# A transformer block, forward and backward, on one core: another hand-set order of the same 1948 operations, and other addresses for their buffers

## The chip, the core and the metric

The kernel runs on one core of a Trainium2 chip. The core has five engines that each work through a queue of their own in order: TensorE (PE in the profile: matmuls, with its weight loads listed as PEld), VectorE (DVE), ScalarE (ACT), GpSimd (POOL) and SyncE (SP), which only issues transfers (DMAs). An instruction that waits for a semaphore holds up everything behind it on its own engine, and nothing on the others until they need its result. The metric is the device time of one execution in microseconds (us).

## What is computed

One pre-LN transformer block on x of 2048 x 512 (S x D), and the gradients of its inputs. The attention has 32 heads of 16, and each position looks at W = 8 positions, 2 apart, behind itself. The feed-forward part has 1792 columns.

```
def _A_ref(x, wqkv, wo):
    W, dil = 8, 2
    ...
    idx = pos[:, None] - off[None, :]
    ...
    logits = jnp.einsum("bhsd,bhswd->bhsw", q, kg) * scale
    ...
    o = jnp.einsum("bhsw,bhswd->bhsd", attn, vg)
    ...
h = x + _A_ref(_layernorm(x, axis=-1), A_wqkv, A_wo)
h2 = h + _B_ref(_layernorm(h, axis=-1), B_w1, B_b1, B_w2, B_b2)
...
_out, _vjp = jax.vjp(_f, A_x, A_wqkv, A_wo, B_w1, B_b1, B_w2, B_b2)
_grads = _vjp(grad_out)
```

The outputs are h2 and the gradients of x, wqkv, wo, w1, b1, w2 and b2.

## The kernel before

**Tiling and stages.** The 2048 positions are cut into four chunks of 512, called chunk 0 to 3 here; the kernel works on them in the order 0, 2, 1, 3 from the attention on. A chunk passes through these stages, all of them interleaved with those of other chunks: load of `xt`; statistics (L360, L361), reciprocal deviation by POOL (L373) and the shift `nm` by DVE (L376); normalization on ACT into `ln`; a DMA that transposes `ln` into `ln1T` (L291); the products with the weights for q and k (L616, in 32-column matmuls) and for v (L268 or L270); evictions from PSUM by ACT (L297: `qt`, `kt`, `tmv`); the band products of q and k on DVE (`prf`, L468, four to a chunk) and their sums by PE (L476); the maximum on DVE (`mx`, L682), its subtraction by PE (L268 or L270, named by `nident`), the exponential on ACT (`e`, L689), its sum by PE (L694), the reciprocal on DVE (`r`, L699), the weights `attn` (L701) and their transposed form `cfo` (L486); the band products with v on DVE (`prbo`, L507, four to a chunk), their sums by PE (L516) and the evictions `ost` (L521); a turn by PE (L532); the product with wo; the first residual `h` on DVE (L739); the second normalization; and the feed-forward products (`ln2T,w` then `w,gl`). In the backward half the same four kinds of band products stand as `prb`, `prbq`, `prbk` and `prbv`, and the gradient of x leaves DVE as `gx` (L559) over `jk`, `u` and `gyr`. The weight gradients are matmuls over all positions, evicted by ACT into `wgs`, `wgso` and `wgsq`, and stored.

**What sets the order.** `Plan` (L55 on) first records all operations, without issuing them: `pl.op` notes the engine, the buffers that are read and written and from them which operation must follow which. `Plan.emit` then issues them in the sequence of the table `ORDER`, a permutation of the 1948 numbers; each engine's queue is the part of it that falls to that engine. There is no scheduler at work beyond that table. A second table, `HOMES`, gives each buffer its address: a place in SBUF in units of 64 bytes, or one of the eight PSUM banks. Two buffers may have the same address one after the other. Then the first operation that writes the later one waits until the last one that uses the earlier one has ended; this is called a wait for an address below.

**What the order also decides.** A matmul of 128 columns is issued as four of 32 columns where the operations beside it are of the 32-column kind, so that PE does not change between the two kinds of layout. `emit` finds those stretches (`quad`), and `mmul` issues them:

```
if pl.quad:
    for a in range(4):
        T.matmul(out[32 * a:32 * a + 32, :], lhsT=l[:, 32 * a:32 * a + 32], rhs=r, start=start, stop=stop, skip_group_check=True)
else:
    T.matmul(out, lhsT=l, rhs=r, start=start, stop=stop, skip_group_check=True)
```

L268 is the first of these two calls and L270 the second, so one and the same product may have either line. SP's queue holds nearly all transfers: loads (L282), stores (L287, L445) and transposes (L291); the gathers of the neighbouring positions (L460) are issued by POOL.

Of the kernel before, what the change touches and what calls it, by code (L numbers as in the profile page):

```python
# [159 lines left out]
def kernel(  # L160
# [1026 lines left out]
    10, 24, 0, 25, 1, 8, 12, 11, 23, 14, 15, 69, 17, 29, 19, 20, 50, 22, 9, 26, 16, 51, 13, 52, 30, 53, 42, 27, 54, 252, 43, 39, 172, 55, 2, 18, 31,  # L1187
    61, 3, 44, 46, 28, 4, 32, 5, 45, 47, 56, 57, 355, 59, 64, 66, 48, 49, 67, 174, 65, 62, 60, 63, 68, 146, 171, 75, 173, 77, 78, 175, 148, 276, 76,
    176, 72, 353, 79, 274, 70, 38, 80, 177, 277, 178, 81, 71, 275, 181, 85, 86, 179, 278, 380, 279, 82, 180, 83, 379, 73, 84, 183, 6, 378, 87, 74,
    377, 88, 89, 280, 92, 381, 110, 382, 90, 284, 91, 105, 96, 283, 102, 93, 354, 97, 184, 94, 383, 112, 98, 99, 281, 95, 7, 100, 194, 597, 108, 195,  # L1190
    282, 101, 21, 189, 286, 196, 188, 114, 192, 250, 182, 190, 456, 109, 387, 111, 217, 191, 37, 386, 126, 285, 113, 193, 115, 185, 384, 116, 117,
    186, 385, 295, 215, 389, 187, 297, 118, 147, 288, 211, 595, 298, 58, 119, 294, 213, 299, 120, 296, 300, 201, 121, 122, 197, 128, 301, 127, 202,
    302, 129, 198, 203, 289, 199, 204, 292, 311, 290, 132, 200, 130, 291, 149, 403, 293, 303, 287, 140, 352, 305, 131, 251, 304, 404, 137, 306, 212,
    307, 214, 216, 205, 141, 314, 598, 133, 142, 138, 134, 218, 139, 405, 135, 318, 143, 136, 406, 408, 332, 480, 144, 152, 208, 316, 388, 156, 458,
    308, 407, 150, 320, 409, 315, 317, 319, 219, 321, 322, 153, 323, 220, 151, 324, 154, 157, 221, 161, 401, 155, 398, 325, 159, 397, 158, 160, 162,
    326, 163, 327, 164, 334, 333, 335, 338, 343, 400, 399, 391, 402, 395, 165, 392, 40, 168, 167, 394, 166, 222, 396, 170, 393, 336, 249, 337, 481,
    41, 414, 339, 596, 340, 341, 529, 342, 346, 507, 344, 508, 515, 345, 390, 223, 229, 347, 145, 224, 535, 348, 231, 351, 517, 419, 533, 518, 519,
    527, 520, 230, 530, 349, 421, 523, 350, 356, 536, 524, 505, 417, 528, 503, 534, 516, 509, 506, 525, 423, 504, 418, 526, 420, 510, 422, 484, 240,
    362, 360, 424, 511, 513, 485, 243, 514, 241, 415, 539, 242, 521, 358, 425, 483, 244, 363, 426, 245, 490, 543, 361, 411, 235, 544, 482, 427, 551,
    123, 246, 416, 232, 552, 599, 537, 236, 547, 247, 357, 410, 540, 364, 237, 494, 233, 359, 259, 234, 365, 531, 257, 366, 238, 367, 428, 239, 548,  # L1200
    368, 258, 369, 263, 255, 248, 370, 169, 253, 373, 374, 541, 256, 371, 262, 549, 372, 429, 559, 376, 254, 545, 261, 568, 435, 260, 553, 457, 264,
    610, 265, 560, 266, 225, 561, 604, 608, 546, 562, 550, 837, 861, 542, 845, 563, 329, 601, 267, 554, 862, 566, 835, 846, 564, 268, 269, 855, 836,
# [118 lines left out]
```

## Time and profile before

| | us |
|---|---|
| median of 3 runs (554.83 to 557.09) | 555.21 |
| the profiled execution, its own time | 555.56 |
| its span, first to last instruction | 553.8 |
| PE busy in it | 534.0 (96%) |
| DVE busy in it | 495.1 (89%) |
| ACT busy in it | 307.2 (55%) |
| POOL busy in it | 24.2 (4%) |
| mean granted TensorE clock, of 1 | 0.995 |

The span is 1.8 us shorter than the execution; times in the rows below are counted from the start of the span. A wait row such as "PE ps L516 <- DVE prbo L507: 3.2, 2, 1.6" says: matmuls of L516 that write PSUM waited for `prbo`, which DVE writes in L507, 3.2 us in all, in 2 places, at most 1.6 us in one. In a timeline, neighbours of one kind stand in one row with their number (x8), the first figure is the start and the second the length of all of them.

### The profile page before, as it was taken

The numbers are of one execution on the slowest core, as the hardware profiler recorded it, in microseconds if no ns is written. First come the engines' busy times: TensorE is split into PE (matmuls) and PEld (weight loads), VectorE is DVE, ScalarE is ACT, GpSimd is POOL, SyncE is SP. The second block draws the span as 40 slices with busy tenths as digits, with TensorE's granted clock in tenths as the row PEclk, the third lists the DMA queues.
The fourth block names the chain that finished last, engine by engine and source line by source line (L and its number), as shares of the span: only waits on it lengthen the run. The fifth ranks groups of instructions, "written<-read, shape, count | busy, mean of one in ns | idle before, by whom it ended". The sixth has DMA issues, their size and how long they took to land. (4 is left out here: it accounts for less than half of the span.)

```text
span 553.8 us, 12777 instructions
## 1 busy us (share of the span) xinstructions
PE 534.0 (96%) x5440; PEld 263.1 (48%) x5440; DVE 495.1 (89%) x649; ACT 307.2 (55%) x480; POOL 24.2 (4%) x38
## 2 busy tenths in 40 slices
PE   8989879999999999999999999999999999999996
PEld 4654434444544444444444445455445445545542
DVE  7999999999999999979993856788979999999993
ACT  3965466989989966987142323223133466652431
POOL 1200001020000100000000000000001001000000
PEclk9999999999999999999999999999999999999999
DMA  8999989997799488998999999999999999938346
GB/s 256 247 291 278 350 248 375 182 276 209 208 263 288 129 203 188 294 266 157 221 184 206 188 225 201 271 188 287 185 363 386 344 367 367 386 86 264 42 125 179
DMA packets 218121, 135.30 MB, mean 244 GB/s; under 512 B 168464, under 2 KB 213712, under 8 KB 216016
## 3 DMA queue, kind: packets, MB, share of 16 engines
q1 hardware_dynamic: 214752, 93.07, 72.8%
q0 software_dynamic: 3312, 41.42, 19.1%
q8 instruction: 42, 0.69, 0.5%
q14 instruction: 15, 0.12, 0.1%
HBM read 55.74 MB, written 39.40 MB: 172 GB/s over the span
## 5 line engine op out<-in xcount | busy, mean ns | idle before, releaser
L270 PE MATMUL ps<-goT,w2T 128*128 128x512 bf16 x220 | 52.5, 379 | 0.6 <-DVE xb L848 0.6
L270 PE MATMUL ps<-w1T,xb 128*128 128x512 bf16 x224 | 51.6, 379 | 0.0
L297 ACT CAST wgs<-ps 128x512 bf16<-128x512 f32 (+1 forms) x30 | 16.4, 558 | 63.1 <-PE ps L268 33.6
L270 PE MATMUL ps<-w,gl 128*128 128x512 bf16 x212 | 48.1, 379 | 0.0
L468 DVE TENSOR_TENSOR prb<-got,vw 128x4096 bf16<-128x4096 bf16 x16 | 36.3, 2282 | 12.2 <-PE ps L270 7.1
L270 PE MATMUL ps<-ln2T,w 128*128 128x512 bf16 x188 | 45.3, 389 | 0.3
L766 ACT ACTIVATE xb<-ps,b1c 128x512 bf16<-128x512 f32 x56 | 35.5, 695 | 10.6 <-PE ps L270 10.4
L848 DVE SCALAR_TENSOR_TENSOR xb<-xb,ps 128x512 bf16<-128x512 bf16 x56 | 36.6, 681 | 4.3 <-PE ps L270 3.8
L507 DVE TENSOR_TENSOR prbq<-Rq,cfq 128x4096 bf16<-128x4096 bf16 x16 | 35.8, 2280 | 2.5 <-PE ps L270 2.1
L507 DVE TENSOR_TENSOR prbv<-Rv,cfv 128x4096 bf16<-128x4096 bf16 x16 | 36.1, 2283 | 1.4 <-PE ps L516 1.3
L507 DVE TENSOR_TENSOR prbo<-Ro,cfo 128x4096 bf16<-128x4096 bf16 x16 | 36.0, 2286 | 0.6 <-PE ps L476 0.5
L507 DVE TENSOR_TENSOR prbk<-Rk,cfk 128x4096 bf16<-128x4096 bf16 x16 | 35.8, 2287 | 0.5 <-PE ps L268 0.3
L468 DVE TENSOR_TENSOR prf<-qt,kt 128x4096 bf16<-128x4096 bf16 x16 | 35.7, 2280 | 0.0
L270 PEld LDWEIGHTS <-xb 128*128 128x128 bf16 x224 | 21.9, 98 | 26.5 <-issue 0.2
L270 PEld LDWEIGHTS <-w2T 128*128 128x128 bf16 x220 | 21.5, 98 | 27.0 <-issue 1.4
L270 PEld LDWEIGHTS <-gl 128*128 128x128 bf16 x212 | 20.7, 98 | 24.6 <-issue 0.2
L616 PE MATMUL ps<-ln1T,wqk 128*32 128x512 bf16 x512 | 30.0, 382 | 1.1 <-ACT ln1T L297 1.1
L788 ACT ACTIVATE xb<-xb 128x2048 bf16<-128x2048 bf16 (+1 forms) x16 | 26.9, 1692 | 6.5 <-DVE xb L787 6.3
L270 PEld LDWEIGHTS <-w 128*128 128x128 bf16 x188 | 18.5, 100 | 23.8 <-issue 4.1
L268 PE MATMUL ps<-gw1in,ln 128*32 128x512 bf16 x496 | 29.1, 379 | 0.0
L784 ACT ACTIVATE x<-xb 128x2048 bf16<-128x2048 bf16 (+1 forms) x16 | 27.0, 1697 | 3.5 <-DMA out_dram<-h2s 2.1
L270 PE MATMUL ps<-gor,gw2in 128*128 128x512 bf16 x120 | 28.5, 379 | 0.0
(194 smaller groups left out, 1008.1 us busy)
## 6 DMA issues: line engine op xcount, KB each, us to landing
Ro<-v_d POOLq DMA_DIRECT2D x4, 2304.0 KB, 12.2
Rq<-k_d POOLq DMA_DIRECT2D x4, 2304.0 KB, 11.4
Rv<-go_d POOLq DMA_DIRECT2D x4, 2304.0 KB, 13.3
Rk<-q_d POOLq DMA_DIRECT2D x4, 2304.0 KB, 14.6
g_d<-gl SPq DMA_DIRECT2D x9, 512.0 KB, 4.1
gh_d<-xb SPq DMA_DIRECT2D x9, 512.0 KB, 3.7
w<-in_B_w_dram SPq DMA_DIRECT2D x2, 1792.0 KB, 13.0
out_dram<-wgs SPq DMA_DIRECT2D x13, 256.0 KB, 4.3
```

The costliest lines, as they stand in the source:

```text
L268: T.matmul(out[32 * a:32 * a + 32, :], lhsT=l[:, 32 * a:32 * a + 32], rhs=r, start=start, stop=stop, skip_group_check=True)
L270: T.matmul(out, lhsT=l, rhs=r, start=start, stop=stop, skip_group_check=True)
L297: fn = lambda: A.copy(out=ap(), in_=pap())
L468: op("DVE", tt_us(4096), lambda g=g, pr=pr: V.tensor_tensor(out=pr(), in0=ql()[:, g, :].unsqueeze(1).to_broadcast([P, W, 512]), in1=_sub(k ...
L507: V.tensor_tensor(out=pr().rearrange("p a j (d h) -> p a j d h", h=H), in0=_sub(R()[:, o0, 0:1], [[st, 2], [512, 4], [32, DH], [1, H]]), i ...
L616: T.matmul(ps()[32 * a:32 * a + 32, gg * 512:(gg + 1) * 512], lhsT=_sub(wq_()[:, dc, 0:1], [[DH, H]], sel * D + 4 * g + a), rhs=rhs, start ...
L766: op("ACT", act_us(512, 1), lambda f=f, ps=ps, xb=xb, f0=f0: A.activation(out=xb()[:, f - f0, :], in_=ps(), func=ACT.Identity, bias=b1c[:, ...
L784: op("ACT", act_us(N), lambda xb=xb, x2=x2: A.activation(out=fl(x2), in_=fl(xb), func=ACT.Square), r=[xb], w=[x2], tag="x2")
L788: op("ACT", act_us(N), lambda xb=xb: A.activation(out=fl(xb), in_=fl(xb), func=ACT.Tanh, scale=GC), w=[xb], tag="tanh", mode=6)
L848: op("DVE", 0.61, lambda f=f, ps=ps, z=z, f0=f0: V.scalar_tensor_tensor(out=z()[:, f - f0, :], in0=z()[:, f - f0, :], scalar=1.0, in1=ps() ...
```

## The change

The operations, their data and their instructions stay; two tables are replaced. In `ORDER` the operations stand in another sequence, and in `HOMES` most buffers have another address. As the neighbours of some 128-column products change, 148 of them instead of 156 stretches are issued in four parts, and PE has 5356 matmuls instead of 5440. DVE, ACT, POOL and SP issue the same instructions as before, in another order.

```diff
 ORDER = (
-    10, 24, 0, 25, 1, 8, 12, 11, 23, 14, 15, 69, 17, 29, 19, 20, 50, 22, 9, 26, 16, 51, 13, 52, 30, 53, 42, 27, 54, 252, 43, 39, 172, 55, 2, 18, 31,
...
 )
...
 HOMES = (
-    1089, 607, 2839, 673, 1185, 2551, 2261, 1473, 549, 2261, 2117, 336, 3159, 3031, 224, 545, 3095, 1957, 1729, 3031, 897, 1089, 1989, 417, 903, 0,
...
 )
```

In the rows that follow, a name such as `prf_110_17_383` is a buffer's name with two counters behind it; only the name ahead of them matters, and that two rows with the same counters share a buffer.

**First place: VectorE, from the shift `nm1` of chunk 2 to that of chunk 3.** `mv1`, `ve1`, `rstd1` and `nm1` belong to the first normalization; `prf` are the products of q and k; `mx` is the maximum of chunk 0. Before:

```order
L376 SCALAR_TENSOR_TENSOR nm1<-mv1,rstd1 128x4
L371 TENSOR_SCALAR ve1<-mv1 128x4
L468 TENSOR_TENSOR prf_110_17_383<-qt0_98_17_351,kt0_11_4_128 128x4096
L650 COPY kt1_122_20_402<-kt0_11_4_128 128x4x16
L376 SCALAR_TENSOR_TENSOR nm1<-mv1,rstd1 128x4
L468 TENSOR_TENSOR prf_125_21_407<-qt0_98_17_351,kt0_11_4_128 128x4096
```

And in the changed kernel:

```order
L376 SCALAR_TENSOR_TENSOR nm1<-mv1,rstd1 128x4
L371 TENSOR_SCALAR ve1<-mv1 128x4
L468 TENSOR_TENSOR prf_101_17_373<-qt0_91_14_350,kt0_14_6_134 128x4096
L468 TENSOR_TENSOR prf_119_18_401<-qt0_91_14_350,kt0_14_6_134 128x4096
L468 TENSOR_TENSOR prf_126_18_427<-qt0_91_14_350,kt0_14_6_134 128x4096
L468 TENSOR_TENSOR prf_136_18_484<-qt0_91_14_350,kt0_14_6_134 128x4096
L468 TENSOR_TENSOR prf_144_19_533<-qt1_138_18_502,kt1_94_15_362 128x4096
L679 TENSOR_TENSOR ps<-ps,mk 32x8x16
L682 TENSOR_REDUCE mx_155_17_582<-ps 128x128
L376 SCALAR_TENSOR_TENSOR nm1<-mv1,rstd1 128x4
```

Between `ve1` and the second `nm1`, which needs what POOL makes of that `ve1`, there was one band product and a copy; now there are five band products, a mask and a maximum.

**Second place: VectorE, from the products with v of chunk 0 to the first residuals.** `prbo` are the products with v, `prf` those of q and k of chunk 2; the two `mx` belong to chunk 1 and to chunk 2, in this order; `h0` is the residual of chunk 0. Before:

```order
L507 TENSOR_TENSOR prbo_195_27_755<-Ro_156_22_556,cfo_190_26_742 128x4096
L507 TENSOR_TENSOR prbo_204_27_801<-Ro_156_22_556,cfo_190_26_742 128x4096
L650 COPY kt2_203_27_799<-kt1_122_20_402 128x4x16
L507 TENSOR_TENSOR prbo_213_26_848<-Ro_156_22_556,cfo_190_26_742 128x4096
L507 TENSOR_TENSOR prbo_220_27_902<-Ro_156_22_556,cfo_190_26_742 128x4096
L468 TENSOR_TENSOR prf_228_22_940<-qt2_182_24_715,kt2_203_27_799 128x4096
L468 TENSOR_TENSOR prf_238_20_980<-qt2_182_24_715,kt2_203_27_799 128x4096
L468 TENSOR_TENSOR prf_248_23_1007<-qt2_182_24_715,kt2_203_27_799 128x4096
L468 TENSOR_TENSOR prf_255_24_1024<-qt2_182_24_715,kt2_203_27_799 128x4096
L682 TENSOR_REDUCE mx_260_22_1052<-ps 128x128
L682 TENSOR_REDUCE mx_262_22_1062<-ps 128x128
L739 TENSOR_TENSOR h0_263_23_1064<-ps,xp0_62_13_207 128x512 x3
```

And in the changed kernel:

```order
L682 TENSOR_REDUCE mx_195_22_792<-ps 128x128
L468 TENSOR_TENSOR prf_198_23_811<-qt2_190_21_763,kt2_178_25_710 128x4096
L507 TENSOR_TENSOR prbo_204_24_864<-Ro_142_18_523,cfo_185_24_743 128x4096
L507 TENSOR_TENSOR prbo_212_23_912<-Ro_142_18_523,cfo_185_24_743 128x4096
L507 TENSOR_TENSOR prbo_220_21_951<-Ro_142_18_523,cfo_185_24_743 128x4096
L507 TENSOR_TENSOR prbo_230_21_994<-Ro_142_18_523,cfo_185_24_743 128x4096
L468 TENSOR_TENSOR prf_240_21_1024<-qt2_190_21_763,kt2_178_25_710 128x4096
L468 TENSOR_TENSOR prf_249_22_1056<-qt2_190_21_763,kt2_178_25_710 128x4096
L468 TENSOR_TENSOR prf_254_23_1068<-qt2_190_21_763,kt2_178_25_710 128x4096
L739 TENSOR_TENSOR h0_259_22_1110<-ps,xp0_147_18_544 128x512 x2
L682 TENSOR_REDUCE mx_263_20_1137<-ps 128x128
L739 TENSOR_TENSOR h0_259_22_1110<-ps,xp0_147_18_544 128x512
```

The maximum of chunk 1 moved from behind these eight products to ahead of them, one `prf` moved ahead of the four `prbo`, and two residuals now stand between the last `prf` and the maximum of chunk 2.

**Third place: SyncE, the last stores.** `gx` are the stores of the gradient of x and `wgsq` those of the gradient of wqkv. Before:

```order
L287 DMA out_1_dram<-gx_1915_17_7263 128x1x512
L287 DMA out_1_dram<-gx_1875_35_7189 128x1x512
L287 DMA out_1_dram<-gx_1915_17_7263 128x1x512
L287 DMA out_1_dram<-gx_1870_35_7179 128x1x512
L287 DMA out_2_dram<-wgsq_1902_20_7240 128x2x512
L287 DMA out_1_dram<-gx_1875_35_7189 128x1x512
L287 DMA out_1_dram<-gx_1915_17_7263 128x1x512 x2
L287 DMA out_1_dram<-gx_1870_35_7179 128x1x512
L287 DMA out_2_dram<-wgsq_1939_10_7315 128x2x512
```

And in the changed kernel:

```order
L287 DMA out_1_dram<-gx_1872_39_7101 128x1x512
L287 DMA out_1_dram<-gx_1874_38_7107 128x1x512 x2
L287 DMA out_2_dram<-wgsq_1802_36_6759 128x2x512
L287 DMA out_2_dram<-wgsq_1922_19_7196 128x2x512
L287 DMA out_1_dram<-gx_1924_19_7199 128x1x512 x3
L287 DMA out_1_dram<-gx_1874_38_7107 128x1x512
L287 DMA out_1_dram<-gx_1924_19_7199 128x1x512
L287 DMA out_2_dram<-wgsq_1942_7_7237 128x2x512
```

The last store is that of a `wgsq` in both. Between it and the `wgsq` store before it stood four stores of `gx`; now five do. On PE, nine groups of four products of the last weight gradient now follow the last product that feeds a `gx`; before, eleven did.

200 rows, old and new, of tables (HOMES, ORDER) are left out of this document.

## The prediction

> **What bounds the kernel now.** I read the page's first part, then the busy times cut into stretches, then the two lists of waits, then single places on the timeline.
>
> ```profile
> span 553.8 us, 12777 instructions
> PE 534.0 (96%) x5440; PEld 263.1 (48%) x5440; DVE 495.1 (89%) x649; ACT 307.2 (55%) x480; POOL 24.2 (4%) x38
> 0.00:40.00 40.00, 36.27 (x452) 21.71 (x453) 36.05 (x66) 27.38 (x38) 6.92 (x12) 1.00 0.92 262
> 40.00:58.00 18.00, 16.15 (x216) 8.08 (x215) 17.89 (x12) 10.60 (x13) 0.02 (x1) 1.00 1.10 290
> 58.00:80.00 22.00, 16.74 (x242) 9.42 (x241) 20.78 (x25) 10.58 (x13) 1.55 (x2) 1.00 0.94 302
> 80.00:113.00 33.00, 32.54 (x322) 15.13 (x323) 32.15 (x32) 26.70 (x34) 1.82 (x4) 0.95 1.00 273
> 113.00:230.00 117.00, 116.02 (x666) 52.73 (x664) 113.53 (x191) 100.97 (x128) 5.93 (x6) 1.00 0.86 227
> 230.00:370.00 140.00, 139.39 (x997) 65.69 (x995) 109.69 (x185) 55.63 (x96) 0.60 (x1) 1.00 1.05 215
> 370.00:554.00 184.00, 176.90 (x2555) 90.32 (x2552) 164.96 (x144) 75.38 (x161) 7.39 (x14) 0.99 0.84 257
> ```
>
> The columns are the length of a stretch, then the busy time of PE, PE's weight loads, DVE, ACT and POOL, then the granted clock, the DMA share and GB/s. PE is the bound: of 553.8 us it is idle for 19.8. No order makes its work shorter, so the change can only be worth what PE idles, plus what the clock holds back, and not all of that. PE's idle time is 3.7, 1.9, 5.3 and 0.5 us in the first four stretches, 1.0 and 0.6 in the next two, and 7.1 in the last, most of which lies behind its last matmul. So there are three places to look: the first 113 us, the waits behind 370, and the tail.
>
> In the first 113 us DVE is nearly as full as PE: it idles 4.0, 0.1, 1.2 and 0.9 us. The waits of both:
>
> ```profile
> PE ps L516 <- DVE prbo L507: 3.2, 2, 1.6
> PE ps L270 <- DVE r L699: 1.6, 1, 1.6
> PE ps L268 <- DVE mx L682: 1.4, 1, 1.4
> PE ps L516 <- DVE prbk L507: 1.1, 1, 1.1
> PE ps L270 <- ACT wgs L297: 0.6, 1, 0.6
> PE ps L516 <- DVE prbv L507: 0.3, 1, 0.3
> DVE mx L682 <- PE ps L476: 0.9, 1, 0.9
> DVE nm L376 <- POOL rstd L373: 0.8, 1, 0.8
> DVE prbo L507 <- PE ps L476: 0.5, 1, 0.5
> ```
>
> PE's three dearest causes in this part are results of DVE: 3.2 + 1.6 + 1.4 = 6.2 us. That they go from the place where they stand is not enough. What counts is when PE last meets DVE:
>
> ```profile
> 138.67 4.49 DVE L507 TENSOR_TENSOR prbo<-Ro,cfo 128x4096 bf16<-128x4096 bf16 x2
> 141.01 0.62 PE L516 MATMUL ps<-prbo,S 128*32 128x512 bf16 x8
> ```
>
> The first of these two products ends halfway, at 138.67 + 4.49/2 = 140.9, and PE's sum of it starts at 141.0. So at 141 PE stands right behind DVE, and every wait of PE before it has only used up slack that this meeting would have taken anyway. What moves the meeting, and with it PE's whole later course, is DVE's own lost time ahead of it.
>
> **The change, part by part.** *DVE's waits ahead of 141.* The wait for POOL (0.8) was that of the second `nm1` in the first place; five products and a maximum now cover POOL's work, so it goes. The wait of `mx` for the sums (0.9) stood ahead of the maximum of chunk 2 in the second place; two residuals now lie ahead of it, so it goes, provided that PE is not later there. The wait of `prbo` (0.5) was one for an address that the sums of the next chunk had just read; with the new homes it has another neighbour, and I count it as gone. Together 0.8 + 0.9 + 0.5 = 2.2 us. The work of DVE that lies ahead of the meetings, less that of PE ahead of the same sums, adds between 0.4 and 0.9 us by counting both queues with the durations of the trace; I take 0.4. Term one: **2.6 us**. Its ends are 0 (a new wait takes all of it) and 2.2 + 0.9 = 3.1.
>
> What hides the edits on PE itself there: that the wait for `r` (1.6, one for a PSUM bank) goes, and that all q, k and v products of chunk 3 but two now stand ahead of the first `prbo` sum of chunk 2, changes where PE idles, not when it meets DVE at 141. PE's waits for `mx` and `prbo`, 1.4 + 3.2 = 4.6 us in three pieces, become about one piece of 5 us at the first sum.
>
> *The change from 128 columns to four times 32.* It costs nothing:
>
> ```profile
> 514.06 0.86 PE ps L268 x16
> 524.87 23.43 PE ps L270 x108
> ```
>
> Sixteen small matmuls take 0.86 us, and four whole ones 23.43 / 27 = 0.87. The 84 fewer matmuls are no time.
>
> *The middle, 113 to 370.* PE idles 1.0 + 0.6 = 1.6 us in 257. I take nothing, with 1.6 gained at one end; at the other a late transfer like that of rival B, which costs up to 2.5.
>
> *Behind 370.* PE waits 1.1 for `prbk`, 0.6 for the eviction of `wgs` (an address) and 0.3 for `prbv`: 2.0 us. In the new order the transposition `cfq`, behind which the wait for `prbk` began, no longer follows the store of a `wgs` that it waits for:
>
> ```profile
> DVE cfq L486 <- DMA out_dram<-wgs: 3.2, 1, 3.2
> ```
>
> So I count 1.1 + 0.3 = 1.4 as gone and let a new wait for some address take the place of the 0.6. Term two: **1.4 us**, between 0 and 2.0.
>
> *The tail.* SP issues the last stores one after the other:
>
> ```profile
> 547.62 2.52 SPq L287 DMA_DIRECT2D out_dram<-gx  x4
> 548.32 0.58 ACT L297 CAST wgsq<-ps 128x512 bf16<-128x512 f32 x1 [2.00 <-PE ps L270]
> 550.24 0.54 SPq L287 DMA_DIRECT2D out_dram<-wgsq  x1
> ```
>
> The last eviction ends at 548.32 + 0.58 = 548.90, and its store is issued at 550.24, because four `gx` stores of 0.63 each stand ahead of it: 1.34 us lost. In the third place five `gx` stores stand ahead, but they can start earlier. The `wgsq` store ahead of them needs an eviction that has five groups of four matmuls behind it on PE (5 x 0.87 = 4.3), so it is free to go 4.3 us ahead of the last eviction's end; five stores take 5 x 0.63 = 3.2, and the last `gx` itself is ready sooner, with nine groups behind its last product instead of eleven only if DVE needs no more than 9 x 0.87 = 7.8 for it. Term three: **1.3 us**, between 0 and 1.3.
>
> *The sum.* 2.6 + 1.4 + 1.3 = 5.3. The profiled execution took 555.56 (its span and 1.8 around it), 0.35 over the median of 555.21. 555.56 - 5.3 = 550.3, and less the 0.35 as a median 549.9. I say **550.0**.
>
> **A rule to weigh: the clock.** Beside the waits for `prbo` the granted clock falls:
>
> ```profile
> 76.77 0.61 PE L516 MATMUL ps<-prbo,S 128*32 128x512 bf16 x8 [1.62 <-DVE prbo L507]
> 78.96 0.61 PE L516 MATMUL ps<-prbo,S 128*32 128x512 bf16 x8 [1.58 <-DVE prbo L507]
> 75.00:80.00 5.00, 1.71 (x23) 1.00 0.83 139
> 80.00:85.00 5.00, 4.72 (x32) 0.66 0.94 285
> 85.00:90.00 5.00, 5.00 (x40) 1.00 1.11 400
> ```
>
> After 5 us in which PE was busy for 1.71, the next 5 us have a clock of 0.66 and then 1.00: a loss of 5 x 0.34 = 1.7 us, as of one spell of 3.4 us at half. Three idle pieces of under 2 us brought it on, and the new order has one of 5 us in their place; so I count one spell before and one after, and no difference.
>
> The Trainium skill's page "TensorE: Matmul & The Clock Gate", section "Part 1: The HAM clock gate", says that an idle window of about 3.4 us halves the clock, and that about 3.4 us of sustained work restore it. The length of the spell agrees; but no single idle piece here was as long as 3.4 us, so by the rule there should have been no spell before, and the piece of 5 us would add one: 550.0 + 1.7 = 551.7, if nothing hides it. The trace, with its spell already there, leaves the sum at 550.0.
>
> **Rivals.** *A: the single long wait costs a spell more than before.* For it: one piece of 5 us, in which PE does nothing at all, where it was busy for 1.71 of 5 before. Against it: with one spell PE comes to the next meetings in time by counting both queues, and of a second spell's 1.7 us some 0.6 would be taken up there. That leaves 1.1: 551.1; if both spells stand in full, 550.0 + 3.4 = 553.4.
>
> *B: the transposed input of chunk 3 comes late.*
>
> ```profile
> 32.44 12.06 SPq L291 DMA_TRANSPOSE ln1T<-ln  x1
> 48.26 1.91 PE L268 MATMUL ps<-wv,ln1T 128*32 128x512 bf16 x32 [0.92 <-DMA ln1T<-ln]
> DMA to landing us min/median/max: 4.5/10.1/15.8
> ```
>
> It was issued at 32.4 and landed 15.8 later, and PE waited 0.9. In the new order the last normalization of chunk 3 stands on ACT behind two evictions of v, so that I place the issue near 38.5: 34.4 us of matmuls end with those that the second eviction needs, PE has idled 3.7 - 1.6 = 2.1 by then (the first stretch without the wait for `r`), and eviction and normalization take about 2. PE asks for the result near 48. With the median of 10.1 it lands at 48.6, and PE waits under 1 us, which is hidden. With 15.8 it lands at 54.3: PE is 6.3 us late, more than the 4 us or so by which DVE's residuals and maximum follow PE's products, and DVE loses 2.5 of the 2.6 of term one: 552.5.
>
> *C: the late waits stay*, as the rings of buffers are shared in new ways: term two is 0, 551.4. With the tail's term at 0 as well, 552.7.
>
> *D: slower.* The mechanism is that of B, with one place and one threshold. Each microsecond that the transposed input lands past about 52 holds up DVE and so the meeting at 141. All other gains, 5.3, are used up if it lands at 57.3, which is 18.8 after its issue; the longest in the trace is 15.8. At 60.5, 22.0 after, it is 3.2 over that of before: 558.4. That SP held it for 12.06 us in its queue before speaks for a queue that can be full; that fewer gathers of x stand ahead of it speaks against.
>
> *E: the order doesn't bind*, so that the meeting at 141 is set by something other than DVE, and only the tail is gained: 553.9, within 0.5% of before.
>
> **How the numbers follow.** A run of this kernel can tell about 0.5%, 2.8 us, from no change: faster is under 552.4, slower over 558.0. Forecast (548.3 to 552.3): 0.50. More gain than that (terms of 3.1, 2.0 and 1.3, and the middle's 1.6: 8.0, or 547.2): 0.09. A 0.11, half of it over 552.4. B 0.10, most of it over. C 0.09, a third over. D 0.05, E 0.06. Faster: 0.50 + 0.09 + 0.06 + 0.03 + 0.06 = 0.74; same: 0.05 + 0.07 + 0.03 + 0.06 = 0.21; slower 0.05. The range leaves out D, part of E and what little lies below the best of the gains: 547.0 to 554.0.
>
> **What would show it.** Term one: the rows of `nm` for POOL and of `mx` for the sums are gone from DVE's waits, and the sum at 141 of chunk 3's products starts 2 to 3 us sooner. Term two: no row of PE for `prbk` over 0.5. Term three: the last store follows the last eviction by under 0.2. A: two stretches of 5 us with a clock under 0.8. B and D: a row of PE for `ln1T` of several us. What would make me wrong is a wait of PE that I don't see between 141 and 370, where it idled 1.6 us in all: the order is new there too, and I price it by its idle time alone.

## The result: 1% slower, where a gain of 1% was predicted

| | before | after |
|---|---|---|
| median, us | 555.07 (6 runs, 553.75 to 565.22) | 559.76 (6 runs, 558.77 to 562.78) |
| ratio, 95% interval | | 1.0102 [1.0076, 1.0127] |
| profiled execution, us | 555.56 | 559.31 |
| mean granted clock | 0.995 | 0.987 |

Ratios, here and below, leave out executions that took over 1.5% longer than the fastest of the same kernel.

The page of the changed kernel, and its busy times in the stretches that the prediction used (columns as there):

```profile
span 557.5 us, 12643 instructions
PE 537.2 (96%) x5356; PEld 264.9 (48%) x5356; DVE 495.4 (89%) x649; ACT 306.6 (55%) x480; POOL 23.7 (4%) x38
0.00:40.00 40.00, 38.20 (x464) 21.59 (x468) 36.82 (x68) 26.79 (x38) 6.92 (x12) 1.00 0.87 255
40.00:58.00 18.00, 17.06 (x259) 10.59 (x252) 17.75 (x11) 12.60 (x16) 1.08 (x2) 1.00 1.02 289
58.00:80.00 22.00, 16.05 (x205) 7.92 (x203) 21.62 (x25) 8.22 (x11) 1.63 (x2) 0.84 0.99 326
80.00:113.00 33.00, 32.93 (x383) 16.16 (x376) 32.44 (x35) 29.27 (x39) 2.14 (x3) 1.00 1.09 272
113.00:230.00 117.00, 116.33 (x668) 52.85 (x667) 111.01 (x187) 103.47 (x137) 3.90 (x4) 1.00 0.91 238
230.00:370.00 140.00, 134.06 (x960) 61.10 (x961) 105.16 (x183) 48.91 (x81) 0.60 (x1) 0.98 1.03 205
```

The line to look at is the last. Before, PE idled 0.6 us between 230 and 370; now it idles 5.9, and the clock is lower too. The first two stretches are better by 1.9 and 0.9 us; the third is worse by 0.7, at a clock of 0.84. PE's and DVE's waits name what is new:

```profile
PE ps L516 <- DVE prbo L507: 4.8, 2, 4.6
PE ps L476 <- DVE glf L919: 4.1, 1, 4.1
PE ps L270 <- DMA ghT<-ghr: 1.5, 1, 1.5
...
DVE prb L468 <- DMA go_d<-tmgod: 8.0, 1, 8.0
...
DVE cfq L486 <- DMA out_dram<-wgs: 2.6, 1, 2.6
...
DVE nm L376 <- POOL rstd L373: 0.9, 1, 0.9
```

The rows of PE for `mx`, `r`, `prbk` and `prbv`, and those of DVE for `mx` and `prbo`, are gone. New on PE are the 4.1 and the 1.5 (and 1.1 for an `e`); of DVE's new waits the 8.0 is the one to follow, since PE comes to wait behind it. The timeline of the same kernel shows how the 8.0 and the 4.1 hang together, and, with the other places that the prediction named:

```profile
74.90 1.04 PE L516 MATMUL ps<-prbo,S 128*32 128x512 bf16 x8 [4.56 <-DVE prbo L507]
189.86 0.16 DVE L376 SCALAR_TENSOR_TENSOR nm<-mv,rstd 128x4 f32<-128x4 f32 x1 [0.93 <-POOL rstd L373]
310.43 3.63 PE L270 MATMUL ps<-ghT,woT 128*128 128x512 bf16 x16 [1.47 <-DMA ghT<-ghr]
350.76 0.61 SPq L287 DMA_DIRECT2D go_d<-tmgod x1
359.98 2.29 DVE L468 TENSOR_TENSOR prb<-got,vw 128x4096 bf16<-128x4096 bf16 x1 [7.97 <-DMA go_d<-tmgod]
362.19 1.22 DVE L919 TENSOR_TENSOR glf<-ps,attn 128x1024 bf16<-128x1024 f32 x1
363.46 1.04 PE L476 MATMUL ps<-prb,S 128*32 128x512 bf16 x8 [4.08 <-DVE glf L919]
550.67 3.18 SPq L287 DMA_DIRECT2D out_dram<-gx  x5
552.67 0.58 ACT L297 CAST wgsq<-ps 128x512 bf16<-128x512 f32 x1 [1.14 <-PE ps L270]
553.95 0.54 SPq L287 DMA_DIRECT2D out_dram<-wgsq  x1
```

In the new `HOMES` one of the four band products `prb` of chunk 2 (operation 1355) lies where `tmgod` lay, which SP stores to `go_d`. The store is issued at 350.76, and DVE can write there only from 359.98 on; nothing of the product's data is missing, as e2 below shows. PE comes to the sums of that product 4.08 us too early (the row names `glf`, which stands behind the product on DVE and reads the bank that the sums write). Behind the wait the clock falls:

```profile
355.00:360.00 5.00, 4.38 (x21) 1.85 (x19) 0.02 (x1) 1.01 (x1) 0.00 (x0) 1.00 1.12 409
360.00:365.00 5.00, 1.54 (x16) 0.67 (x19) 4.97 (x4) 0.28 (x1) 0.00 (x0) 0.73 1.01 264
365.00:370.00 5.00, 5.00 (x60) 2.08 (x56) 3.86 (x3) 0.00 (x0) 0.00 (x0) 0.59 0.62 129
370.00:375.00 5.00, 5.00 (x80) 3.10 (x73) 4.89 (x5) 1.50 (x2) 0.00 (x0) 1.00 1.03 219
```

0.62 + 3.46 us idle, then 5 x 0.41 = 2.05 us of clock: about 6.1 in one place.

To lay the kernels side by side I count, for each matmul, its start less the durations at full clock of all the work that stands ahead of it in PE's queue: how far PE is **behind its own work**, after so many us of it (the last column is the end). Each row is the one profiled execution of its kernel.

| us of PE's work done | 140 | 280 | 320 | 380 | 523 |
|---|---|---|---|---|---|
| before | 17.7 | 18.7 | 18.8 | 20.2 | 23.3 |
| after | 15.5 | 16.7 | 18.7 | 26.1 | 27.7 |
| e19, the last experiment | 15.1 | 16.3 | 21.2 | 21.5 | 23.1 |

By 280 the new order has gained 2.0. From 280 to 320 it loses 2.0 where before lost 0.1: 1.9 given back (the wait for `ghT`, and some clock). From 320 to 380 it loses 7.4 against 1.4: 6.0. From 380 on it loses 1.6 against 3.1: 1.5 gained. The tail is 0.6 better. -2.0 + 1.9 + 6.0 - 1.5 - 0.6 = 3.8, and the two profiled executions differ by 559.31 - 555.56 = 3.75.

### The profile page after: what moved, and what is told of

The parts are those of the page before. It is cut to its first block, busy times and chain, and to the rows that moved or that the text cites. A ratio compares the mean times of both kernels' runs of the same rounds, so it can differ in the third digit from the quotient of the medians.

```text
span 557.5 us, 12643 instructions
## 1 busy us (share of the span) xinstructions
PE 537.2 (96%) x5356; PEld 264.9 (48%) x5356; DVE 495.4 (89%) x649; ACT 306.6 (55%) x480; POOL 23.7 (4%) x38
## 4 chain that ended last, share of the span: by engine, by line
PE 60%; DVE 10%; DMA 3%; issue 2%; SPq 1%; ACT 0%; DVEq 0%
PE ps L270 35%; PE ps L268 19%; PE ps L516 4%; DVE xb L848 2%; DMA go_d<-tmgod 2%; PE ps L476 1%; DVE prbo L507 1%; PE ps L532 1%; DVE x L791 1%; DVE xb L795 1%; DMA ghT<-ghr 1%; DVE x L792 1%; DVE ga L785 1%; DVE xb L787 1%; DVE x L789 1%
## 5 line engine op out<-in xcount | busy, mean ns | idle before, releaser
L270 PE MATMUL ps<-w,gl 128*128 128x512 bf16 x216 | 50.1, 379 | 0.2 <-DVE h2s L820 0.2
L468 DVE TENSOR_TENSOR prb<-got,vw 128x4096 bf16<-128x4096 bf16 x16 | 36.0, 2282 | 11.7 <-DMA go_d<-tmgod 8.0
L270 PE MATMUL ps<-ln2T,w 128*128 128x512 bf16 x180 | 41.2, 379 | 0.0
L788 ACT ACTIVATE xb<-xb 128x2048 bf16<-128x2048 bf16 (+1 forms) x16 | 27.0, 1691 | 20.2 <-DVE xb L787 20.1
L616 PE MATMUL ps<-ln1T,wqk 128*32 128x512 bf16 x512 | 31.4, 389 | 0.1
L270 PE MATMUL ps<-gor,gw2in 128*128 128x512 bf16 x112 | 26.6, 379 | 0.0
L769 ACT ACTIVATE gl<-xb 128x2048 bf16<-128x2048 bf16 (+1 forms) x16 | 26.6, 1686 | 0.0
## 6 DMA issues: line engine op xcount, KB each, us to landing
Ro<-v_d POOLq DMA_DIRECT2D x4, 2304.0 KB, 11.7
```

The costliest lines, as they stand in the source:

```text
L468: op("DVE", tt_us(4096), lambda g=g, pr=pr: V.tensor_tensor(out=pr(), in0=ql()[:, g, :].unsqueeze(1).to_broadcast([P, W, 512]), in1=_sub(k ...
L616: T.matmul(ps()[32 * a:32 * a + 32, gg * 512:(gg + 1) * 512], lhsT=_sub(wq_()[:, dc, 0:1], [[DH, H]], sel * D + 4 * g + a), rhs=rhs, start ...
L769: op("ACT", act_us(N), lambda xb=xb, gl=gl: A.activation(out=fl(gl), in_=fl(xb), func=ACT.Gelu_apprx_tanh), r=[xb], w=[gl], tag="gelu", mo ...
L788: op("ACT", act_us(N), lambda xb=xb: A.activation(out=fl(xb), in_=fl(xb), func=ACT.Tanh, scale=GC), w=[xb], tag="tanh", mode=6)
```

## The experiments

Diffs show SP's part of `ORDER`, by the number of the operation and a name; where `HOMES` changes, its entry. Unless a line says otherwise, an experiment starts from the changed kernel. A transfer "lands" when its completion is seen in the trace. There is no e10.

**Is it that one store?** `tmstgo` 1352 is the store of `tmgod`, `tmxgo` 1351 the transposition ahead of it. It goes far ahead (e1), a little ahead (e2), and one place back (e3).

In e1:

```diff
+1351 tmxgo
 1798 gwin1
+1352 tmstgo
 1708 gwin2
-1351 tmxgo
...
-1352 tmstgo
```

In e2:

```diff
 1469 fmgh
+1352 tmstgo
 1772 gwin1
 1706 wgst2
-1352 tmstgo
```

In e3:

```diff
-1352 tmstgo
 1821 gwin1
+1352 tmstgo
```

> The changed kernel with four transfers of SP in another order around 335 us: the transposition into tmgod of chunk 2 and its store to go_d stand ahead of two loads for weight gradients instead of behind them. Theory (the band product prb waits for the address that this store frees, PE waits for it, and PE's idle time halves its clock): the store is issued near 342 instead of 350.8 and has landed before DVE asks at 352; DVE's wait of 8.0 us falls under 1, PE's wait of 4.1 for L476 under 0.5, the granted clock of 360 to 380 is 1.00 instead of 0.83. Time 559.8 - 4.1 - 3.2 = 552.5. Rival (PE's own order puts the sum sr behind DVE's maximum too late, so the DVE chain is late anyway): PE still waits over 2 us near 360, time over 556.

> The changed kernel with only the store to go_d of chunk 2 moved ahead of one load and one store on SP: issued near 347.0 instead of 350.8. Theory: it lands near 356, DVE waits about 4 us instead of 8, but PE asks for the product only at 359.4, so that half of DVE's wait costs PE nothing: PE's wait under 1 us, no half clock, time 552.5 to 553.5. Rival (each microsecond of DVE's wait is a microsecond of the kernel): 559.8 - 4 = 555.8.

> The changed kernel with the store to go_d of chunk 2 moved behind one more load on SP: issued near 355.6, 4.8 us later. Theory: DVE waits 12.8 us, PE 8.9, one to one as there is no slack left: 559.8 + 4.8 = 564.6, and up to 566.3 if the clock loses another spell. Rival (the time comes from elsewhere): within 1 us of 559.8.

Measured: e1 1.0072 [1.0042, 1.0101] of before, e2 1.0068 [1.0042, 1.0094], e3 1.0149 [1.0107, 1.0191]. The waits of e3, then of e2:

```profile
PE ps L476 <- DVE glf L919: 7.8, 1, 7.8
DVE prb L468 <- DMA go_d<-tmgod: 11.7, 1, 11.7
```

```profile
PE ps L476 <- DVE prb L468: 5.2, 1, 5.2
DVE prb L468 <- issue: 6.7, 1, 6.7
```

In e3 the store is issued at 351.19, only 0.4 later and not the 4.8 that were expected, but DVE can write from 362.3 on, 2.3 later, and had asked 1.4 sooner: its wait is 3.7 longer, PE's 3.7, and the kernel's median 2.6 (the two intervals overlap). The edit alone does not explain this, since in e4 and e6 below, where the store keeps its place, DVE waits 10.8 and 11.0 and PE 6.9 and 7.1. What the four executions show together is that PE's wait is DVE's wait less 3.9 in each (8.0 and 4.1, 10.8 and 6.9, 11.0 and 7.1, 11.7 and 7.8): PE is late by as much as that address is. And with the store early (e2: issued 346.2, landed 351.1) this product waits 0.21 in place of 7.97, so the store is the cause of its wait. Yet e1 and e2 both miss the 552.5 to 553.5 that was expected, as most of PE's wait is still there. It is now that of the next product, whose address belonged to a `wgs` buffer, and the store of that one landed at 363.4 (the row says "issue", as the profile names no releaser). So the first wait had covered a second. Nearly the same price, another address.

**The second address, and the early `ghT`.** e5 is e2 with another address for that `wgs` buffer, e6 the address alone; e7 is e5 with the load of `ghT` (1217) ahead of two loads that are needed 70 us later; e4 moves the store of `h2s` (1056) up, for which DVE's `u` had waited 3.1.

The address in e5 and e6, in `HOMES`:

```diff
-2544
+1505
```

In e7:

```diff
+1217 fmgh
 1136 gwin1
 1113 gwin1
-1217 fmgh
```

In e4:

```diff
 1732 gwin2
+1056 h2st
...
 1122 gwin1
-1056 h2st
```

> The changed kernel with the last of four stores of h2s issued near 282 instead of 296.8 on SP; its data are ready at 275.4, and u takes the address that it frees. DVE's wait of 3.1 us for it should go in any case. Theory (this wait makes ghr late, so the transposition into ghT, so PE): PE's wait of 1.5 for ghT falls under 0.3 and the time to 558.3. Rival (SP's queue, with two loads ahead of that transposition, is what makes ghT late): PE's wait falls by at most 0.7, time 559.1 to 559.8.

> e2_go_store_sooner and, beside it, one number of HOMES: the buffer wgs of one weight gradient (128x1024) gets an address of its own place (119360 instead of 185856 bytes), so that the band product prb after next no longer takes the address that its store frees. Theory now (two waits of prb for addresses lay one behind the other: for the store to go_d, and for the store of wgs; e2 freed the first only): DVE's wait of 6.7 us for prb falls under 1, PE's wait of 5.2 us for L476 under 0.5, the stretch 345 to 380 has the clock at 1.00. Time 558.2 - 5.2 - 0.9 = 552. Rival (a third wait of the same kind lies behind these two): over 556.

> The changed kernel with that one number of HOMES alone, and its order as it was. Theory: prb still waits 8.0 us for the store to go_d, and the second wait, which lay behind it, was free by then (365.5 against 364.1): PE's wait stays near 4 us, time 558.8 to 559.8. Rival (the wgs address is the whole cause): PE's wait gone, time near 552.

> e5_store_and_home, and the transposition into ghT of chunk 1 ahead of two loads for weight gradients on SP instead of behind them. Theory: it is issued as soon as DVE's ghr is done, near 303.5 instead of 305.3, and PE's wait of 0.8 to 1.5 us for ghT falls under 0.3: 1 us less than e5, 551. Rival (its time to land grows by what it was issued earlier, since the loads ahead of it are still under way): no difference to e5.

Measured: e4 1.0116 [1.0069, 1.0162], e5 1.0116 [1.0068, 1.0165], e6 1.0115 [1.0075, 1.0155], e7 1.0042 [1.0007, 1.0076]. In e4 `u` waits 3.3 for `c` in place of 3.1 for the store: nothing won. PE's wait for `ghT` falls from 1.5 to 0.8 by it, as its rival said. e6 shows that the second address alone is worth nothing while the first stands. e5 has no wait for `prb` on PE any more, and still no gain, since a third thing was hidden behind the two. PE's waits in e5, then in e7:

```profile
PE ps L268 <- DMA gw1in<-gh_d: 8.9, 1, 8.9
```

```profile
PE ps L268 <- DMA gw1in<-gh_d: 5.6, 1, 5.6
PE ps L516 <- DVE prbo L507: 5.0, 3, 4.6
PE ps L268 <- DMA ghT<-ghr: 2.5, 1, 2.5
```

The load `gw1in` 1747 is issued at 374.8 in both, and PE goes on only at 387 and at 385; before, it was issued at 361.8, landed at 366.3 and was used at 379.4. In e7 the load of the next `ghT` is late as well, by 2.5. Its ratio is below that of e5 by 0.7%, where 1 us was expected, but the intervals just overlap.

**Does the long idle piece at 70 to 75 cost clock?** e8 is e5 and 36 matmuls on constants, which nothing reads, in PE's longest idle place at 70 to 75.

```diff
+def mmf():
+    for _ in range(36):
+        T.matmul(pz2()[:, 0:P], lhsT=ident[:], rhs=ident[:], start=True, stop=True)
```

> e5_store_and_home with 36 pairs of a weight load and a matmul of 128 columns on constants put into PE's queue ahead of the first sum of prbo of chunk 2, where PE idles 4.6 us at 70 to 75; their product is not used. Theory (the one long idle piece halves the clock for one or two spells of 3.4 us, and DVE's later work hides that): the clock of 58 to 80 rises from 0.84 or 0.92 to 1.00, PE is ahead by 1.7 to 3.4 us at 90, but by under 1 us at 230, and the time is 0 to 1 under that of e5. Rival A of the prediction (the spells are not hidden): the time is 1.1 to 3.4 under that of e5.

Measured: 1.0105 [1.005, 1.0161], as e5. Between 70 and 80 the clock stays at 1.00, where the changed kernel had 0.72 and 0.60 and e5, whose queues are the same there, 0.97 and 0.69. At 80 us of work PE is 1.1 less behind than in e5. Later in that execution PE waited 6.0 for a late transposed `ln2T`, so whether the 1.1 reaches the end is open.

**All late loads last.** The order of SP holds loads that are needed 90 to 160 us later ahead of those that PE is about to need. e9 puts four of them behind; e11 adds the edits of e7.

```diff
-1003 wqkvT
-1000 wqkvT
-1002 wqkvT
-1798 gwin1
...
 1773 gwin1
+1798 gwin1
...
 1849 r16ro
+1002 wqkvT
+1000 wqkvT
+1003 wqkvT
```

> The changed kernel with four transposing loads moved back on SP and nothing else: one of gw1in that PE uses at 423 us but that is issued at 335.9, and three of wqkvT, used at 452 and issued at 290, 297 and 323; they go behind 383 and 407. New theory (the waits of prb, of gw1in and of ghT are one thing: SP's queue and the transfers are full from 290 to 390, and loads that nobody needs yet stand ahead of those that are due): 3.2 + 1.5 us of SP's time go from between 320 and 351, so that the store to go_d is issued near 346 and lands near 351 to 355, the store of wgs near 352 and lands by 357, the load gw1in of chunk 1 (374.3) near 367 and lands by 376, before PE asks at 378 to 385. PE's waits for L476 and for gw1in are under 1.5 us in all, time 552 to 554. Rival (only the homes count): PE's waits over 4 us, time over 557.

> e9_late_loads_last and all of e7_store_home_ght (store to go_d sooner, the new address of wgs, the transposition into ghT ahead of two loads). By the new theory all four places of waiting behind 290 are free: 1 to 1.5 us under e9, 551 to 552.5, that is 2 to 4 under the kernel before. Rival (a further transfer comes late in their place): no better than e9.

Measured: e9 1.0303 [1.0246, 1.0361], e11 1.0351 [1.0296, 1.0405]. Both miss, by far. As far as 400 the theory holds: after 380 us of work PE is 17.8 behind in e9, less than before's 20.2. Then PE waits for a single `gw1in` load, 34.9 us in e9 and 19.4 in e11.

**Loads by when they are due.** e12 leaves those four where they were and only swaps neighbours on top of e7: 1747 ahead of 1771 and of a transposition. e13 also lets `ghT` 1344 go ahead of `gw2in` 1684.

In e12:

```diff
+1748 gwin1
+1747 gwin1
 1771 gwin1
-1748 gwin1
...
-1747 gwin1
```

Added in e13:

```diff
+1344 fmgh
 1684 gwin2
-1344 fmgh
```

> e7_store_home_ght with two loads of the SP queue put in the order in which PE needs them: the weight-gradient load gw1in (operation 1747, needed by PE first, at about 379) now goes ahead of gw1in 1771 (needed at about 400) and ahead of the transposition of chunk 3, instead of behind both. In e7 it was issued at 374.8 and landed about 384; its address is free from 363.4. Theory (a few named transfers stand behind others that are due later): it is issued at about 367.5, lands before 377, the PE wait of 5.6 for gw1in goes, the half-clock spell behind it too (380 to 390 had a clock of 0.66), and the kernel comes to 552 to 555, ratio 0.995 to 1.000. Rival (transfers there are crowded as a whole, so a load served sooner makes another late): a wait of 3 or more comes up for another transfer between 360 and 410, and the kernel stays at 558 or more.

> e12_loads_by_due, and the gw2in load 1684 (needed at about 331) behind the transposed load of ghT for the next chunk (1344, needed at about 317) instead of ahead of it. In e7 that ghT landed at 319.7 and PE waited 2.5 for it. Theory: that wait goes as well, and the kernel comes about 2.5 below e12, to 550 to 553, below the kernel before. Rival (crowded as a whole): the load put back, or one behind it, is late in its place by about as much, and the time is that of e12 within 1.

Measured: e12 1.0368 [1.0287, 1.045], e13 1.0447 [1.0389, 1.0504]. In e12 PE has no wait over 0.2 between 340 and 400; 1747 landed at 374.8. What came in its place is far over what either side expected: 27.8. First SP and POOL on the timeline of e12, then the windows (the clock is the third figure from the right, GB/s the last):

```profile
398.70 3.59 SPq L291 DMA_TRANSPOSE gw1in<-gh_d  x1
...
405.35 21.59 SPq L291 DMA_TRANSPOSE gw1in<-gh_d  x1
...
405.19 0.53 POOL L460 DMA_DIRECT2D Rq<-k_d  x1 [24.96 <-DVE prbv L507]
...
440.83 1.86 PE L270 MATMUL ps<-gw1in,ln 128*128 128x512 bf16 x4 [27.81 <-DMA gw1in<-gh_d]
```

```profile
410.00:415.00 5.00, 2.97 (x43) 1.26 (x37) 2.99 (x4) 0.60 (x1) 1.07 (x2) 1.00 1.00 332
415.00:420.00 5.00, 0.00 (x0) 0.00 (x0) 0.44 (x1) 0.00 (x0) 0.00 (x0) 0.81 1.31 126
420.00:425.00 5.00, 0.00 (x0) 0.00 (x0) 0.00 (x0) 0.00 (x0) 0.00 (x0) 0.50 1.18 84
425.00:430.00 5.00, 0.00 (x0) 0.00 (x0) 0.00 (x0) 0.00 (x0) 0.00 (x0) 0.50 1.13 48
```

Two transposing loads of one kind: the first held SP for 3.59 us, the second, issued 0.16 after POOL's gather, for 21.59. From 420 on all engines stand still, and the transfers move 48 to 126 GB/s at a full DMA share. In the changed kernel, whose gather started 5.3 after the load, the windows of 5 us from 415 to 430 have 392 to 424. What moved them together is the repair itself: the gather goes out when DVE's product `prbv` is done, and with DVE no longer held up it goes out at 405.2 instead of 407.4 in the changed kernel, while the load, at the same place in SP's queue, goes out at 405.35 instead of 402.1.

**Load and gather apart, and together on purpose.** e14 puts 1796 and 1797 ahead of what nothing needs before 430. e15 is the kernel before with 1797 moved to where POOL's gather starts. e16 and e17 were to take the last `wqkvT` load (1001) behind the gathers.

In e14, from e12:

```diff
-1846 r16ro
 1720 wgst2
-1848 r16ro
 1773 gwin1
-1001 wqkvT
 1796 gwin1
+1797 gwin1
...
-1797 gwin1
+1846 r16ro
+1848 r16ro
+1001 wqkvT
```

In e15, from the kernel before:

```diff
-1797 gwin1
 1796 gwin1
...
 1849 r16ro
+1797 gwin1
```

In e16, from e14 (e17 has the swap of e13 as well):

```diff
 1797 gwin1
+1759 wgst1
...
+1849 r16ro
 1001 wqkvT
-1759 wgst1
-1849 r16ro
```

> e12_loads_by_due, and on SP's queue the gw1in loads 1796 and 1797 of 398 to 405 go ahead of three small loads, a wqkvT load and three stores (1846, 1848, 1001, 1847, 1845, 1834, 1770), which nothing needs before 430. In e12 load 1797 was issued at 405.3, 0.1 after POOL began the gather of chunk 2 (405.2), its issue held SP until 426.9, it landed at 440.8, and PE waited 27.8 for it. Theory (a gw1in load that is issued while POOL's gathers run takes over 20 instead of 5 to 7): 1797 is issued at about 399, lands by 406 ahead of the gathers, the wait goes, and the kernel is at 550 to 555. Rival 1 (the load is late for another reason, its place behind the others in the queue): it lands late whenever it is issued and the wait stays. Rival 2 (the collision moves on): another gw1in load or the gathers' own data are late by over 5, and the kernel stays above 558.

> The kernel before, with one load moved: gw1in 1797, issued there at 395.4 (landed 400.7, needed by PE at 411.6), goes behind the small load 1849 on SP's queue, so that it is issued at about 405, just after POOL begins a gather (404.7). Theory (load and gathers in each other's way): it takes over 20, PE waits 15 or more, and the kernel comes to 570 or more. Rival (only the place in the queue counts): it lands at about 411 to 413, PE waits 1 at most, and the time is that of before within 2.

> e14_load_before_gathers, and on SP's queue the wqkvT load 1001 (needed at about 455) goes from just ahead of POOL's gathers to behind them, and the store 1759, whose buffer the gather takes over, goes ahead of the other stores. In the profiled run of e14 load 1001 was caught together with the gather (issued 399.7, landed 422.6), the gather of chunk 2 landed at 425.5 (after: 419.1) and the sums that need it had PE wait 4.1 and about 7 in all between 418 and 440. Theory (a large load issued together with the gathers delays both): with 1001 away the gathers land by 420, those waits go, and the kernel comes to 551 to 553.5, ratio about 0.996. Rival (the gathers alone fill the transfers there): the gathers land as late as in e14 and the time is that of e14 within 1.

> e16_gathers_free, and the gw2in load 1684 behind the transposed load of ghT for the next chunk, as in e13. In e14 PE waited 2.1 for that ghT and a half-clock spell of about 1.8 followed at 320 to 340. Theory: ghT lands before PE is there, the 2 to 4 go, and the kernel comes 2 to 4 below e16, to about 549 to 551: the gain that was predicted for the order, with the middle freed of its late transfers. Rival (what is put back is late by as much, as in e13, where a wait of 2.9 for prb came in its place): within 1 of e16.

Measured: e14 0.9986 [0.9956, 1.0016], e15 1.0032 [0.9992, 1.0072], e16 1.0535 [1.0492, 1.0579], e17 1.0301 [1.0257, 1.0344]. e14 is as the theory said: 1797 landed at 398.5, the wait went, and against the changed kernel that is some 1.2% less (0.9986 to 1.0102). (Its profiled execution took 563.56; the median of 13 is 554.07, and one took 1448.19, which nothing here explains.) e15 missed: 1797 was issued 2.1 ahead of the gather, landed after 10.9, and PE waited 1.7, not 15. In e16 and e17 the edit did not do what it was meant to. SP does not wait for a gather, so 1001 was simply issued at the very moment of it. SP and POOL in e16:

```profile
400.66 23.22 SPq L291 DMA_TRANSPOSE wqkvT<-in_A_wqkv_dram  x1
...
401.36 0.53 POOL L460 DMA_DIRECT2D Rq<-k_d  x1 [24.26 <-DVE prbv L507]
```

That makes it a good test: another load, another matrix, and again SP is held for over 20 us. (PE's longest wait there is one of 24.5 for `prbk`, whose gathered data came late.) Over the profiled executions of all kernels, the transposing loads nearest to the first gather behind 395:

| kernel, load | issued ahead of the gather | held SP | landed after |
|---|---|---|---|
| before, `wqkvT` 1000 | 3.4 | 1.5 | 4.9 |
| after, `gw1in` 1797 | 5.3 | 4.5 | 6.9 |
| e3, 1797 (e1, e2, e4 to e8: between 5.0 and 6.7 ahead, 5.7 to 7.4) | 4.8 | 3.8 | 5.9 |
| e18, 1797 (e19: 7.5 ahead, 6.3) | 5.0 | 3.5 | 5.6 |
| e15, 1797 | 2.1 | 4.3 | 10.9 |
| e14, `wqkvT` 1001 | 2.1 | 3.1 | 22.9 |
| e16, 1001 | 0.7 | 23.2 | 67.9 |
| e17, 1001 | 0.7 | 25.3 | 53.3 |
| e11, 1797 | 0.3 | 8.8 | 27.4 |
| e9, 1797 | 0.1 | 15.6 | 42.8 |
| e12, 1797 | -0.2 | 21.6 | 35.4 |
| e13, 1797 | -1.3 | 29.4 | 38.7 |
| e11, `wqkvT` 1002 | -14.8 | 14.8 | 19.2 |
| e9, 1002 | -21.3 | 23.8 | 28.1 |

At this gather, a load issued 3.4 us or more ahead lands within 7.4. At 2.1 it takes 11 or 23, and from 0.7 ahead to well after the gather's start 19 to 68. The row of e11 is from an ordinary execution (576.74, of 569.41 to 576.87).

But a start close to a gather is not enough. The same traces have single gathers, near 350 and 380, with transposing loads as close:

| kernel, load | issued ahead of a single gather | held SP | landed after |
|---|---|---|---|
| before, `gw1in` at 377.6 | 0.6 | 2.1 | 13.6 |
| before, `gw1in` at 348.9 | -1.0 | 9.7 | 13.3 |
| e9, `vw` at 350.4 | -0.3 | 8.6 | 13.2 |
| e11, `vw` at 354.1 | -0.4 | 8.0 | 12.3 |
| e15, `gw1in` at 379.0 | 0.9 | 2.0 | 8.4 |

These are slower than 5 to 7 us, but there is no stall of 19 to 68. One thing that differs: behind 395 a second gather follows 7.1 us after the first in e9, e11 to e14, e16 and e17, and in six of these seven it is this second one that lands late, after 24 to 47 us, where it takes 10 to 13 in e1 to e8; the first one lands after 10 to 14 in five of them. At the single gathers the next is 23 us or more away. Whether the second gather is the condition was not tried.

**Every transposing load away from the gathers.** e18 puts 1001 early (and the store 1759 ahead of other stores, as in e16); e19 mends the late `ghT` as well, by the swap of e13.

In e18, from e14:

```diff
 1720 wgst2
+1001 wqkvT
 1773 gwin1
...
 1797 gwin1
+1759 wgst1
...
-1001 wqkvT
-1759 wgst1
```

> e14_load_before_gathers, with the transposing wqkvT load 1001 put early on SP's queue, ahead of gw1in 1773 (issue at about 387), so that no transposing load is issued between 396 and the end of the gather that POOL begins at about 401; the store 1759 goes ahead of the other stores as in e16. In e16 load 1001 did not go behind the gathers as was meant: it was issued at 400.7, 0.7 ahead of the gather (401.4), held SP for 23.2 and landed at 468.6. Theory (a transposing load issued at the moment of the gather stalls both, as 1797 did in e9, e11, e12 and 1001 in e14, e16, e17): no wait over 3 for a load or a gather after 400, and the time is that of e14's best runs or below, 551 to 553.5. Rival (the gathers alone are slow there, or another transfer takes the place): a wait of 5 or more between 400 and 440 and a time of 555 or more.

> e18_transposed_early, and the gw2in load 1684 behind the transposed load of ghT for the next chunk (as in e17). Theory: the wait of 2.1 for ghT and the half-clock spell behind it go, 2 to 4 below e18, 548 to 551: the predicted gain of the new order, with the middle freed. Rival: a wait of 2.5 to 2.9 for prb takes the place, as in e13 and e17, and the time is that of e18 within 1; or POOL's gather now meets another transposing load, and it is 565 or more.

Measured: e18 1.0010 [0.9969, 1.0052], e19 1.0001 [0.9976, 1.0025]. No stall at the gathers in either: in e18 the load 1797, issued at 396.9, landed at 402.5, and the gather began at 401.9. But e19 is not 2 to 4 below e18, and neither is below before. The waits of PE in e19, then DVE and PE on its timeline, and the windows there:

```profile
PE ps L516 <- DVE prbo L507: 5.1, 3, 4.6
PE ps L476 <- DVE prb L468: 2.7, 1, 2.7
```

```profile
327.66 2.29 DVE L468 TENSOR_TENSOR prb<-got,vw 128x4096 bf16<-128x4096 bf16 x1 [2.30 <-PE ps L476]
...
330.00 0.77 PE L476 MATMUL ps<-prb,S 128*32 128x512 bf16 x8 [2.73 <-DVE prb L468]
```

```profile
325.00:330.00 5.00, 2.27 (x44) 1.00 (x37) 2.70 (x3) 0.47 (x2) 0.00 (x0) 1.00 1.13 244
330.00:335.00 5.00, 5.00 (x64) 2.49 (x67) 5.00 (x4) 0.02 (x1) 0.00 (x0) 0.66 1.42 257
```

DVE waits 2.30, then PE waits 2.73 for DVE, and 1.7 of clock follow. That is the rival's case: the wait for `ghT` had covered it. The row names PE's sum L476 as what DVE waited for, but that sum stands behind this product (operation 1230) in `ORDER`, and it ended at 327.27, while DVE's wait for its semaphores ended at 327.61. What landed just then, at 327.58, is a transposition, 1131, that reads `xb` at the very address that the product is to write:

```profile
321.23 3.68 SPq L291 DMA_TRANSPOSE xw1in<-xb  x1
```

In e13 and e17 the product starts just behind the same landing as well (328.17 after 328.09, 329.37 after 329.29); in the changed kernel 1131 landed at 325.35 and the product, at 326.35, did not wait. So this is once more an address that a late transfer frees. In the table of PE's lag, e19 is 2.4 ahead of before at 280, 2.4 behind at 320 and 0.2 ahead at the end.

## Why the prediction was wrong

**The step that failed** is "The middle, 113 to 370 ... I take nothing", with a late transfer of at most 2.5 at its bad end. It measured 1.9 + 6.0 = 7.9 lost between 280 and 380 us of PE's work: DVE's wait of 8.0 for the address that a store had to free, PE's 4.1 behind it, some 2.1 of clock behind that, and 1.5 for `ghT`. I had priced that part by PE's idle time before, 1.6 in 257, as if a stretch without waits stayed one in any order. The row of idle time could not show how near the stretch was to waiting. The DMA share of 1.05 in the same row was a hint, but not more than that: the stretch from 40 to 58 has 1.10. The 2.5 at the bad end was itself taken from rival B, where 6.3 less 4 is 2.3. The text named this place as what would make it wrong, and left the range at 554.0 all the same.

**Term one, the start: right, a little smaller.** 2.6 predicted, 2.2 measured at 140 us of work, 2.0 left at 280. The waits for `mx` and `prbo` are gone from DVE, and so is that of `nm` at its place; a wait of 0.93 for POOL came up at 189.9, in a later normalization. PE's small waits did become one piece, 4.56 for the 5 that were foreseen. DVE's own idle time in the first 113 us, which the term was built on, fell from 6.1 to 4.4. One sign was off: the sum at 141 starts at 139.93, 1.1 sooner and not 2 to 3, because 1.1 us more of PE's work now stands ahead of it. PE still stands right behind DVE there, whose product ends at 139.8.

**Term two, the waits behind 370: right.** 1.4 predicted, 1.5 measured. There is no row of PE for `prbk` or `prbv`. e19, which is not late at 380, loses the same 1.6 from there on, so this is not a gift of PE's being late.

**Term three, the tail: half.** 1.3 predicted, 0.6 measured. The last eviction ends at 552.67 + 0.58 = 553.25 and its store is issued at 553.95, 0.70 late for 1.34 before. The five `gx` stores did take 3.2, but started at 550.67, not 4.3 us ahead of the eviction's end.

**The clock: one spell before and, as far as it costs, one after.** The sign of rival A did come: two stretches of 5 us under 0.8 (0.72 and 0.60). 0.84 over 22 us is 3.5 of lowered clock, but 1.4 of it (5 x 0.28) fell between 70 and 75, where PE idled. The fill of e8 shows that it comes from that idle piece. This is what the Trainium skill's page "TensorE: Matmul & The Clock Gate", section "Part 1: The HAM clock gate", says of an idle window of about 3.4 us. That it would add to a spell before, and so cost 1.7 more, did not show in the lag at 140. And so long a piece is not needed: in e19 one of 2.73 has a spell behind it (0.66 over 5 us), as the three short pieces had in the kernel before.

**The rivals.** B and D did not happen: no row of PE for `ln1T`. C and E did not: terms one and two are there. The slower case came true by another mechanism than D's. Of D's kind, a transfer that lands too late, it is; but what is late is a store whose address is wanted, and in the middle.

**Why repairs did not bring the 5.3 back.** Three waits stood one behind the other on that path: the address of `tmgod` (8.0 on DVE, 4.1 on PE), the address of `wgs` (6.7, 5.2), the load 1747 (5.6 to 8.9 on PE). Removing one showed the next; removing all three moved a load and POOL's gathers together, for 27.8. Only with that load moved too (e14, e18, e19) is the kernel level with before. In e19 the gain of the start, 2.4 at 280, meets the band products at 320, where DVE waits for an address that the transposition 1131 still reads, and PE for DVE. That this last wait is the whole of what is missing was not tried. The gain of the start is real, but what PE wins there it can keep only where the stretch behind has room.

## What to carry to other kernels

A stretch in which an engine does not idle is not a stretch with room: before an order or an address is changed there, look at each buffer's new neighbour, at when the neighbour's last reader ends, and, if that reader is a store, at when the store lands in the new queue. When one wait is removed and the time stays, look for the next wait at the same place before the theory is dropped; here there were three, and a fourth when they were gone. And when an engine becomes earlier, ask which transfers it triggers and what they will run into.

## What the hardware showed that I had not expected

At one place, the gather behind 395, a transposing load that was issued between 0.7 us ahead of it and 1.3 behind it held SP for 9 to 29 us and landed after 27 to 68, where loads issued 3.4 us or more ahead of it land after 5 to 7. In e12 the traffic fell to between 48 and 126 GB/s at a DMA share above 1. With the two loads that had met it issued earlier (e18, e19) the stall is gone. A near start alone does not make it: at single gathers of the same traces such loads land after 8 to 14. Nor is a near start needed, since loads issued 15 and 21 us after the gather, while the second one was under way, took 19 and 28. What in the two makes it so was not tried.

The Trainium skill's page "DMA: Bandwidth & Descriptors", section "Issuing engines are not separate DMA queues", says that transfers started by SP and by POOL run on the same 16 DMA engines and interleave. That they share them fits. But sharing alone would lengthen the load by the gather's time, and not lower the sum of both to a third or less of the 392 to 424 GB/s of the changed kernel, nearly all of which was the gathers' (385 on average from 415 to 430). The size varies from run to run: e12's runs lie between 574.48 and 592.41, its profiled one at 587.06.
